# Attention's normalising factor: spread to 128 columns by GpSimd and transposed with the exponentials, instead of spread by fp32 matmuls

## The chip, the cores and the metric

The kernel runs on one core of one Trainium2 chip. Five engines work side by side: TensorE (PE; its weight loads are shown apart as PEld), VectorE (DVE), ScalarE (ACT), GpSimd (POOL) and SyncE (SP), which issues most transfers. TensorE writes only to PSUM, which has eight banks of 128 partitions x 512 fp32 columns; GpSimd cannot read PSUM. The metric is the device time of one execution in microseconds, from the first to the last instruction; shown are three executions and one more that was profiled.

## What is computed

A chain of three blocks on a batch of 4 sequences of 768 rows: a gated linear recurrence (8 heads of 48), a causal attention with 4 experts of 64 columns, of which each row takes the best two, and a layer-normed MLP of width 1536 with a residual.

```python
for t in range(S):                                   # 1: recurrence
    state = alpha[:, :, t, :, None] * state + np.einsum('bhd,bhe->bhde', k[:, :, t], v[:, :, t])
    y[:, :, t] = np.einsum('bhd,bhde->bhe', q[:, :, t], state)
...
    scores = np.where(causal, -1000000000.0, scale * (q @ k.transpose(0, 2, 1)))   # 2: for each expert e
    scores = scores - scores.max(-1, keepdims=True)
    a = np.exp(scores)
    a /= a.sum(-1, keepdims=True) + 1e-09
    ye = a @ v @ wo[e]
    out += mask[..., None] * w[:, :, kk:kk + 1] * ye
...
ch = np.maximum(xn @ w_ch1, 0.0) @ w_ch2             # 3: MLP, xn is the layer norm of x
return x + ch
```

## The kernel before

The program is written as one list of Python calls; a scheduler inside the framework then sets the order of the instructions on each engine, by its own estimate of when each can run, and sets the waits. A change in one function therefore moves instructions of others.

The main loop (line 714) runs over 48 *units* `(b, i, p)`: batch b, query chunk i of 128 rows (0 to 5; in the last batch from 5 down to 0), pair p of two experts. Around each unit `fill` (line 703) pulls in other work: in the first three batches the recurrence and the q, k, v projections of later rows (`front`), in the last batch the MLP of rows that are done (`back`). After the last unit only the MLP remains.

A unit has three parts. `scores(u)` (line 412) is called two units ahead (`LA = 2`). It multiplies q and k (three products of split operands, line 432), takes row maxima on VectorE (lines 438, 440) and exponentials on ScalarE (line 442), which also sums each row into `den`. VectorE inverts `den` (lines 446 to 449), and GpSimd multiplies it with the expert's weight from `W`: `rr`, one number for each row and expert, 128x2 (line 451).

`transp(u)` (line 454) transposes the 2(i+1) blocks of exponentials `A` with TensorE, four to a PSUM bank (line 464), and copies each bank into the buffer `at`; ScalarE does the copy, or VectorE for every fourth (lines 467, 469). `at` has two buffers (`NAT = 2`). The first group is issued ahead of the next `scores`, the rest behind it.

`av(u)` (line 472) multiplies the values `V` with the transposed blocks, so that the result has 64 rows for each expert and a column for each query row (line 487). The factor of a query row must then multiply a column. For that, two more fp32 matmuls (line 490) take `rr` with its one column repeated 64 times as weights and the identity as the moving operand, and so write the factor, spread over 64 partitions, beside the result in the same bank. ScalarE copies it out of PSUM to `rb` (line 493), VectorE multiplies the result with it (line 494), and ScalarE and GpSimd split the product into the parts `oh` and `ol` (lines 495, 496), which `wout` (line 498) multiplies with the output weights one pair of units later.

All PSUM banks come from one pool of eight, `psF`, taken in turn: a bank goes to its next user when the last reader of its contents is done.

When the third batch ends (line 716) the first rows for the MLP and its weights are loaded, and `mlp_ln` (line 581) queues the layer-norm statistics (line 590, BN_STATS of the tile `xt`) on VectorE, where they stand among the attention's instructions.

Of the kernel before, what the change touches and what calls it, by code (L numbers as in the profile page):

```python
# [10 lines left out]
F32 = mybir.dt.float32  # L11
# [4 lines left out]
AF = mybir.ActivationFunctionType  # L16
OP = mybir.AluOpType
# [7 lines left out]
NAT = 2  # L25
MB = 1.0
MB0 = -10000
TM = 4
# [27 lines left out]
B, H, S, D = 4, 8, 768, 48  # L56
DM = H * D
# [14 lines left out]
def kernel(ctx: ExitStack, tc: tile.TileContext, akq, vd, wqkv, wo, g_ln, w1, w2, out):  # L72
    nc = tc.nc
    pe, dve, act, pool, sp = nc.tensor, nc.vector, nc.scalar, nc.gpsimd, nc.sync
# [3 lines left out]
    aw = ctx.enter_context(tc.tile_pool(name="aw", bufs=3))  # L78
    sm = ctx.enter_context(tc.tile_pool(name="sm", bufs=6))
# [58 lines left out]
    ident = const.tile([128, 128], F32, name="ident")  # L138
    make_identity(nc, ident)
    for _ in range(NWU // 4):  # L140
        P = psf()
# [33 lines left out]
            load_wo()  # L175

    def load_wo():
        oraw = aw.tile([128, 2 * S], F32, name="at", bufs=NAT)[:, :2 * DM].rearrange("p (k c) -> p k c", k=2)
        sp.dma_start(oraw, wo)
        act.activation(OWH, oraw, AF.Copy)  # L180
        pool.tensor_tensor(OWL, oraw, f(OWH), op=OP.subtract)
# [230 lines left out]
    def scores(u):  # L412
        b, i, p = UN[u]
# [33 lines left out]
        else:  # L447
            dve.tensor_scalar(den, den, 1e-9, None, op0=OP.add)
        dve.reciprocal(den, den)
        rr = sm.tile([128, 2], F32, name="rr")  # L450
        pool.tensor_tensor(rr, den, W[:, i, 2 * p:2 * p + 2], op=OP.mult)
        RR[u] = rr

    def transp(u):
        b, i, p = UN[u]
        A = AA.pop(u)
        at = aw.tile([128, 2 * S], F32, name="at", bufs=NAT)
        ATT[u] = at
        blk = [(h, x) for h in range(2) for x in range(i + 1)]
        for x0 in range(0, len(blk), 4):  # L460
            g = blk[x0:x0 + 4]
            P = psf()
            for n, (h, x) in enumerate(g):
                pe.transpose(P[:, 128 * n:128 * n + 128], A[h][:, 128 * x:128 * x + 128], ident)  # L464
            cs = slice(128 * x0, 128 * (x0 + len(g)))
            if (u + x0 // 4) % TM:
                act.activation(at[:, cs], P[:, :128 * len(g)], AF.Copy)  # L467
            else:
                dve.tensor_copy(at[:, cs], P[:, :128 * len(g)])
            yield  # L470

    def av(u):
        b, i, p = UN[u]
        V = GEN[b][4]
        if p == 0:
            OT[u // 2] = (aw.tile([128, 2, 128], FR, name="oh", bufs=2), aw.tile([128, 2, 128], FR, name="ol", bufs=2))
        oh, ol = OT[u // 2]
        P = psf()
        rr = RR.pop(u)
        at = ATT.pop(u)  # L480
        O = P[:, 128:256]
        with tc.manual_schedule(engines={mybir.EngineType.PE}):
            for x in range(i + 1):
                for h in range(2):
                    e = 2 * p + h
                    c = 128 * (h * (i + 1) + x)
                    pe.matmul(O[64 * h:64 * h + 64, :], V[:, x, HD * e:HD * e + HD], at[:, c:c + 128],  # L487
                              start=(x == 0), stop=(x == i), skip_group_check=True)
            for h in range(2):
                pe.matmul(P[64 * h:64 * h + 64, :128], rr[:, h:h + 1].to_broadcast([128, 64]), ident, start=True, stop=True,  # L490
                          skip_group_check=True)
        rb = aw.tile([128, 128], F32, name="rb", bufs=2)
        act.activation(rb, P[:, :128], AF.Copy)
        dve.tensor_tensor(rb, O, rb, op=OP.mult)  # L494
        act.activation(oh[:, p], rb, AF.Copy)
        (dve if OLE else pool).tensor_tensor(ol[:, p], rb, f(oh[:, p]), op=OP.subtract)

# [324 lines left out]
```

## Time and profile before

| | us |
|---|---|
| three executions | 744.76, 748.21, 753.51 |
| median | 748.21 |
| the profiled execution, span | 749.8 |
| TensorE busy in it | 713.5 |
| VectorE, ScalarE, GpSimd busy | 447.5, 308.5, 174.5 |

In the rows further down, "busy" of TensorE counts the union of its records; a record's length includes its way through the array, so records overlap, and the start of the next one tells what one costs. fp32 matmuls appear as two records each, transposes as one. A wait is idle time of an engine, put down to what ended it. Line numbers are those of the kernel before; in the changed kernel, lines from 461 to 491 shift by up to 4, and those behind `av` by one.

### The profile page before, as it was taken

The numbers are of one execution on the slowest core, as the hardware profiler recorded it, in microseconds if no ns is written. First come the engines' busy times: TensorE is split into PE (matmuls) and PEld (weight loads), VectorE is DVE, ScalarE is ACT, GpSimd is POOL, SyncE is SP. The second block draws the span as 40 slices with busy tenths as digits, with TensorE's granted clock in tenths as the row PEclk, the third lists the DMA queues.
The fourth block names the chain that finished last, engine by engine and source line by source line (L and its number), as shares of the span: only waits on it lengthen the run. The fifth ranks groups of instructions, "written<-read, shape, count | busy, mean of one in ns | idle before, by whom it ended". The sixth has DMA issues, their size and how long they took to land.

```text
span 749.8 us, 16242 instructions
## 1 busy us (share of the span) xinstructions
PE 713.5 (95%) x6520; PEld 643.2 (86%) x6520; DVE 447.5 (60%) x1241; ACT 308.5 (41%) x879; POOL 174.5 (23%) x284
## 2 busy tenths in 40 slices
PE   7599799989989999999899999999999999999998
PEld 6488678868868788779678888999999999999997
DVE  6757787767897787766678954254245335433521
ACT  3324455545555555555567545232223123212310
POOL 4624345243464334321223221000000000000000
PEclk8688999999999999999999999999999999999999
DMA  8113424233322622211932311001100100110100
GB/s 338 71 57 115 151 68 138 98 117 121 121 97 96 208 61 83 77 41 54 323 99 79 96 43 55 22 32 43 43 11 33 43 22 22 43 43 12 32 22 22
DMA packets 30427, 60.87 MB, mean 81 GB/s; under 512 B 2960, under 2 KB 19856, under 8 KB 30352
## 3 DMA queue, kind: packets, MB, share of 16 engines
q1 hardware_dynamic: 18864, 45.68, 18.3%
q10 hardware_dynamic: 8352, 9.44, 3.6%
q0 software_dynamic: 3136, 4.72, 2.3%
q8 instruction: 51, 0.84, 0.5%
q14 instruction: 24, 0.20, 0.1%
HBM read 45.67 MB, written 14.16 MB: 80 GB/s over the span
## 4 chain that ended last, share of the span: by engine, by line
PE 69%; DVE 9%; DMA 7%; ACT 4%; POOL 3%; issue 3%; SPq 0%; ACTq 0%; POOLq 0%; DVEq 0%
PE F L631 21%; PE F L648 20%; PE F L304 5%; PE F L487 5%; PE F L432 4%; PE F L464 3%; DMA ld<-in_akq_dram 3%; PE F L505 2%; DMA raw<-in_w_dram 2%; DVE gt L199 2%; PE F L263 2%; PE F L318 2%; PE F L221 1%; ACT A L442 1%; PE F L244 1%
## 5 line engine op out<-in xcount | busy, mean ns | idle before, releaser
L635 ACT ACTIVATE hh<-F 128x256 fp32r<-128x256 f32 x144 | 55.0, 384 | 196.6 <-PE F L631 196.0
L631 PE MATMUL F<-nh,w1hl 128*128 128x256 f32 x864 | 129.0, 284 | 0.0
L631 PEld LDWEIGHTS F<-nh,w1hl 128*128 128x128 f32 x864 | 114.4, 191 | 1.7 <-issue 0.7
L648 PE MATMUL F<-w2h,hh 128*128 128x384 f32 x288 | 98.8, 343 | 0.0
L648 PE MATMUL F<-w2l,hh 128*128 128x384 f32 x288 | 97.0, 337 | 0.0
L648 PE MATMUL F<-w2h,hl 128*128 128x384 f32 x288 | 96.9, 336 | 0.0
L636 DVE SCALAR_TENSOR_TENSOR hl<-F,hh 128x256 fp32r<-128x256 f32 x144 | 60.1, 419 | 56.8 <-ACT hh L635 56.3
L442 ACT ACTIVATE A<-F,nm 128x384 f32<-128x384 f32 (+4 forms) x128 | 68.4, 541 | 52.7 <-DVE nm L440 44.4
L652 DVE TENSOR_TENSOR xt<-F,xt 128x384 f32<-128x384 f32 x24 | 13.4, 558 | 110.5 <-PE F L648 110.5
L631 PE MATMUL F<-nl,w1hl 128*128 128x256 f32 x432 | 75.5, 283 | 0.0
L487 PE MATMUL F<-at,V 128*64 128x128 f32 x672 | 62.1, 286 | 2.3 <-ACT at L467 1.6
L631 PEld LDWEIGHTS F<-nl,w1hl 128*128 128x128 f32 x432 | 62.2, 192 | 0.2 <-issue 0.2
L487 PEld LDWEIGHTS F<-at,V 128*64 128x64 f32 x672 | 41.5, 137 | 19.1 <-issue 7.5
L464 PE MATMUL F<-ident,A 128*128 128x128 f32 x336 | 54.5, 284 | 3.3 <-DVE rb L494 2.6
L648 PEld LDWEIGHTS F<-w2h,hh 128*128 128x128 f32 x288 | 54.2, 188 | 1.1 <-issue 0.8
L648 PEld LDWEIGHTS F<-w2l,hh 128*128 128x128 f32 x288 | 54.2, 188 | 0.2
L648 PEld LDWEIGHTS F<-w2h,hl 128*128 128x128 f32 x288 | 54.1, 188 | 0.2 <-issue 0.2
L464 PEld LDWEIGHTS F<-ident,A 128*128 128x128 f32 x336 | 37.9, 142 | 12.6 <-issue 5.0
L221 PE MATMUL F<-ld 48*128 48x128 f32 x384 | 37.8, 309 | 9.1 <-issue 5.1
L221 PEld LDWEIGHTS F<-ld 48*128 48x128 f32 x384 | 30.2, 203 | 15.4 <-issue 9.8
L206 POOL TENSOR_TENSOR ld<-ld,gt 128x512 f32<-128x512 f32 (+1 forms) x26 | 30.2, 1166 | 56.4 <-DVE gt L199 29.1
L467 ACT ACTIVATE at<-F 128x512 f32<-128x512 f32 (+1 forms) x72 | 38.7, 542 | 6.6 <-PE F L464 4.8
(185 smaller groups left out, 1420.9 us busy)
## 6 DMA issues: line engine op xcount, KB each, us to landing
ld<-in_akq_dram SPq DMA_DIRECT2D x24, 770.0 KB, 4.8
vb<-in_vd_dram SPq DMA_DIRECT2D x24, 256.0 KB, 2.8
raw<-in_w_dram SPq DMA_DIRECT2D x18, 256.0 KB, 2.7
wsc<-whl ACTq DMA_DIRECT2D x18, 256.0 KB, 2.4
xs<-xo ACTq DMA_DIRECT2D x24, 192.0 KB, 1.9
w1hl<-wsc POOLq DMA_DIRECT2D x4, 1152.0 KB, 14.9
xt<-xs SPq DMA_DIRECT2D x24, 192.0 KB, 2.5
raw<-in_w_dram SPq DMA_DIRECT2D x12, 384.0 KB, 3.2
```

Source lines behind the costliest of these rows:

```text
L206: (dve if GQ else pool).tensor_tensor(q[:, js], q[:, js], gt[:, js, 1:], op=OP.mult)
L221: pe.matmul(P[h][:, j], k[r, j], q[r, j], start=True, stop=True)
L304: pe.matmul(P[:, mt % 2], wt[:, k, cs], x[:, k], start=(n == 0), stop=(n == 8))
L432: pe.matmul(P[h][x], qt[rs[h], p, qs], kt[rs[h], p, pw * x:pw * x + pw], start=(n == 0), stop=(n == 2), skip_group_check=True)
L442: act.activation(A[h][:, pw * x:pw * x + pw], t, AF.Exp, bias=nm[:, h:h + 1], scale=1.0 if x < npc - 1 else -1.0, accum_out=dn2[:, h, x:x ...
L464: pe.transpose(P[:, 128 * n:128 * n + 128], A[h][:, 128 * x:128 * x + 128], ident)
L467: act.activation(at[:, cs], P[:, :128 * len(g)], AF.Copy)
L487: pe.matmul(O[64 * h:64 * h + 64, :], V[:, x, HD * e:HD * e + HD], at[:, c:c + 128], start=(x == 0), stop=(x == i), skip_group_check=True)
L631: pe.matmul(P, w[:, k, c], x[:, k], start=(n == 0), stop=(n == 8))
L635: act.activation(hh, P, AF.Relu)
L636: dve.scalar_tensor_tensor(hl, P, 0.0, f(hh), op0=OP.max, op1=OP.subtract)
L648: pe.matmul(P, x[:, o], w[:, ff], start=(ff == 0 and n == 0), stop=(ff == KF - 1 and n == 2))
```

## The change

`rr` becomes 128 x 2 x 64: GpSimd writes the product of `den` and the weight 64 times for each expert (line 451 in both kernels), into four buffers of its own. `transp` adds this tile as one more 128x128 block behind the exponentials' blocks, so that its transpose lands in 128 further columns of `at`; and the blocks are now cut into groups of nearly equal size instead of fours and a rest. The number of groups is 1, 2, 2, 3, 3, 4 for i = 0 to 5, against 1, 1, 2, 2, 3, 3. `av` loses the two spreading matmuls and the copy to `rb`; VectorE multiplies the result with the columns of `at`.

```diff
@@ -175,7 +175,7 @@
             load_wo()
 
     def load_wo():
-        oraw = aw.tile([128, 2 * S], F32, name="at", bufs=NAT)[:, :2 * DM].rearrange("p (k c) -> p k c", k=2)
+        oraw = aw.tile([128, 2 * S + 128], F32, name="at", bufs=NAT)[:, :2 * DM].rearrange("p (k c) -> p k c", k=2)
         sp.dma_start(oraw, wo)
         act.activation(OWH, oraw, AF.Copy)
         pool.tensor_tensor(OWL, oraw, f(OWH), op=OP.subtract)
@@ -447,23 +447,27 @@
         else:
             dve.tensor_scalar(den, den, 1e-9, None, op0=OP.add)
         dve.reciprocal(den, den)
-        rr = sm.tile([128, 2], F32, name="rr")
-        pool.tensor_tensor(rr, den, W[:, i, 2 * p:2 * p + 2], op=OP.mult)
+        rr = sm.tile([128, 2, 64], F32, name="rr", bufs=4)
+        pool.tensor_tensor(rr, den[:, :, None].to_broadcast([128, 2, 64]),
+                           W[:, i, 2 * p:2 * p + 2, None].to_broadcast([128, 2, 64]), op=OP.mult)
         RR[u] = rr
 
     def transp(u):
         b, i, p = UN[u]
         A = AA.pop(u)
-        at = aw.tile([128, 2 * S], F32, name="at", bufs=NAT)
+        at = aw.tile([128, 2 * S + 128], F32, name="at", bufs=NAT)
         ATT[u] = at
-        blk = [(h, x) for h in range(2) for x in range(i + 1)]
-        for x0 in range(0, len(blk), 4):
-            g = blk[x0:x0 + 4]
+        blk = [A[h][:, 128 * x:128 * x + 128] for h in range(2) for x in range(i + 1)]
+        blk.append(RR.pop(u).rearrange("p h e -> p (h e)"))
+        ng = (len(blk) + 3) // 4
+        cut = [len(blk) * n // ng for n in range(ng + 1)]
+        for y, (x0, x1) in enumerate(zip(cut, cut[1:])):
+            g = blk[x0:x1]
             P = psf()
-            for n, (h, x) in enumerate(g):
-                pe.transpose(P[:, 128 * n:128 * n + 128], A[h][:, 128 * x:128 * x + 128], ident)
-            cs = slice(128 * x0, 128 * (x0 + len(g)))
-            if (u + x0 // 4) % TM:
+            for n, a in enumerate(g):
+                pe.transpose(P[:, 128 * n:128 * n + 128], a, ident)
+            cs = slice(128 * x0, 128 * x1)
+            if (u + y) % TM:
                 act.activation(at[:, cs], P[:, :128 * len(g)], AF.Copy)
             else:
                 dve.tensor_copy(at[:, cs], P[:, :128 * len(g)])
@@ -476,9 +480,8 @@
             OT[u // 2] = (aw.tile([128, 2, 128], FR, name="oh", bufs=2), aw.tile([128, 2, 128], FR, name="ol", bufs=2))
         oh, ol = OT[u // 2]
         P = psf()
-        rr = RR.pop(u)
         at = ATT.pop(u)
-        O = P[:, 128:256]
+        O = P[:, :128]
         with tc.manual_schedule(engines={mybir.EngineType.PE}):
             for x in range(i + 1):
                 for h in range(2):
@@ -486,12 +489,8 @@
                     c = 128 * (h * (i + 1) + x)
                     pe.matmul(O[64 * h:64 * h + 64, :], V[:, x, HD * e:HD * e + HD], at[:, c:c + 128],
                               start=(x == 0), stop=(x == i), skip_group_check=True)
-            for h in range(2):
-                pe.matmul(P[64 * h:64 * h + 64, :128], rr[:, h:h + 1].to_broadcast([128, 64]), ident, start=True, stop=True,
-                          skip_group_check=True)
         rb = aw.tile([128, 128], F32, name="rb", bufs=2)
-        act.activation(rb, P[:, :128], AF.Copy)
-        dve.tensor_tensor(rb, O, rb, op=OP.mult)
+        dve.tensor_tensor(rb, O, at[:, 256 * (i + 1):256 * (i + 1) + 128], op=OP.mult)
         act.activation(oh[:, p], rb, AF.Copy)
         (dve if OLE else pool).tensor_tensor(ol[:, p], rb, f(oh[:, p]), op=OP.subtract)
```

The scheduler has set the order anew. Two places at the end of the third batch show it. First TensorE, where the kernel before has the last transposes of unit 33 (tiles `A_4858`, `A_4859`) and the first ones of unit 34 (`A_5012`), which go into the bank `F_5160`; `F_5138` is the result of unit 33, `F_5170` to `F_5172` are scores of unit 36. Before:

```order
L464 MATMUL F_5128<-ident_107,A_4858 128x128
L464 MATMUL F_5128<-ident_107,A_4859 128x128 x3
L464 MATMUL F_5134<-ident_107,A_4859 128x128 x2
L487 MATMUL F_5138<-at_5087,V0_377 64x128
L464 MATMUL F_5160<-ident_107,A_5012 128x128 x4
L487 MATMUL F_5138<-at_5087,V0_377 64x128 x6
L432 MATMUL F_5170<-KH1_1409,QH1_1407 128x384
L432 MATMUL F_5170<-KH1_1409,QL1_1408 128x384
L432 MATMUL F_5170<-KL1_1410,QH1_1407 128x384
L487 MATMUL F_5138<-at_5087,V0_377 64x128 x3
L490 MATMUL F_5138<-ident_107,rr_4888 64x128 x2
```

and after the change, where the same units have the tiles `A_4825`, `A_4826` and `A_4979`, the result `F_5105` and the bank `F_5124`:

```order
L468 MATMUL F_5093<-ident_107,A_4825 128x128 x2
L468 MATMUL F_5093<-ident_107,A_4826 128x128 x2
L468 MATMUL F_5099<-ident_107,A_4826 128x128 x3
L468 MATMUL F_5099<-ident_107,rr_4855 128x128
L490 MATMUL F_5105<-at_5053,V0_377 64x128
L468 MATMUL F_5124<-ident_107,A_4979 128x128 x3
L490 MATMUL F_5105<-at_5053,V0_377 64x128 x4
L432 MATMUL F_5133<-KH1_1400,QH1_1398 128x384
L432 MATMUL F_5133<-KH1_1400,QL1_1399 128x384
L432 MATMUL F_5133<-KL1_1401,QH1_1398 128x384
L490 MATMUL F_5105<-at_5053,V0_377 64x128 x5
```

The two matmuls with `rr` and the identity behind the last AV matmuls are gone, a transpose of `rr` stands with the last blocks instead, and the first group of unit 34 has three transposes instead of four. In both kernels the bank `F_5160` or `F_5124` held the result of unit 32 before, so these transposes wait for VectorE's multiplication of that result.

Second VectorE, at the same time, with that multiplication (`rb<-F,rb`, in the change `rb<-F,at`) and the four BN_STATS of the MLP's first rows. Before (the first BN_STATS stands three rows further up):

```order
L438 TENSOR_REDUCE mx_5102<-F 128x1
L449 RECIPROCAL den<-den 128x2
L338 TENSOR_REDUCE rank<-gt__4997 128x8
L590 BN_STATS bs<-xt 128x6
L438 TENSOR_REDUCE mx_5102<-F 128x1
L590 BN_STATS bs<-xt 128x6
L339 SCALAR_TENSOR_TENSOR ex<-rank,ex 128x8
L591 BN_AGGR mv<-bs 128x2
L494 TENSOR_TENSOR rb<-F,rb 128x128
L590 BN_STATS bs<-xt 128x6
L440 ISA F,nm<-F,cmask,mx_5102 128x384
L440 ISA nm 128x1
```

and after the change (here the first row is the first BN_STATS):

```order
L589 BN_STATS bs<-xt 128x6
L449 RECIPROCAL den<-den 128x2
L338 TENSOR_REDUCE rank<-gt__4964 128x8
L589 BN_STATS bs<-xt 128x6
L493 TENSOR_TENSOR rb<-F,at 128x128
L590 BN_AGGR mv<-bs 128x2
L589 BN_STATS bs<-xt 128x6
L440 ISA F,nm<-F,cmask,mx_5067 128x384
L440 ISA nm 128x1
L339 SCALAR_TENSOR_TENSOR ex<-rank,ex 128x8
```

Before, the multiplication stands behind the third BN_STATS, and the maxima of the next scores (`F,nm<-F,cmask`) behind the fourth. After, the multiplication stands behind the second, and the maxima behind the third.

## Rows read from the trace of the kernel before

**Rows 1.** The page: busy time with shares; TensorE in 40 slices of the span
```profile
PE 713.5 (95%) x6520; PEld 643.2 (86%) x6520; DVE 447.5 (60%) x1241; ACT 308.5 (41%) x879; POOL 174.5 (23%) x284
...
PE   7599799989989999999899999999999999999998
```

**Rows 2.** Busy us of each engine (x records) by stretch, then granted clock, DMA
```profile
75.00:470.00 395.00, 377.76 (x3982) 314.23 (x3981) 293.07 (x845) 212.03 (x622) 140.45 (x234) 0.98 0.33 105
368.00:373.00 5.00, 5.00 (x35) 3.80 (x32) 3.23 (x18) 3.37 (x14) 0.01 (x1) 0.66 1.32 389
470.00:750.00 280.00, 276.17 (x1954) 275.80 (x1952) 104.40 (x304) 70.58 (x202) 0.00 (x0) 1.00 0.09 30
```

**Rows 3.** TensorE's waits, 75 to 470 us: us in total, times, longest us
```profile
PE F L304 <- ACT xh L286: 4.2, 2, 3.5
PE F L464 <- DVE rb L494: 2.6, 2, 2.4
...
PE F L432 <- ACT at L467: 1.6, 1, 1.6
PE F L487 <- ACT at L467: 1.6, 4, 1.0
PE F L263 <- DVE rb L494: 1.1, 1, 1.1
...
PE F L244 <- ACT at L467: 0.4, 1, 0.4
PE F L487 <- DVE rb L494: 0.3, 1, 0.3
```

**Rows 4.** By line: duration ns min/median/max, first and last start us
```profile
L490 PE MATMUL F<-ident,rr x192: 272/273/421, 75.3 to 468.1; 128*64 128x128 f32 x192
L464 PE MATMUL F<-ident,A x336: 270/273/477, 63.7 to 465.4; 128*128 128x128 f32 x168
```

**Rows 5.** Timeline of TensorE, 303 to 306 us: start us, us, what xcount
```profile
303.42 0.44 PE L487 MATMUL F<-at,V 128*64 128x128 f32 x4
303.69 0.39 PE L490 MATMUL F<-ident,rr 128*64 128x128 f32 x4
304.00 1.16 PE L244 MATMUL F<-vb,kt 128*128 128x128 f32 x8
305.00 0.60 PE L464 MATMUL F<-ident,A 128*128 128x128 f32 x4
305.53 0.43 PE L263 MATMUL F<-smk,vb 128*32 128x128 f32 x8
```

**Rows 6.** Timeline of TensorE, 259 us, twelve records of AV
```profile
259.15 0.88 PE L487 MATMUL F<-at,V 128*64 128x128 f32 x12
```

**Rows 7.** Groups by line and form: xcount | busy us, mean ns | idle before
```profile
L467 ACT ACTIVATE at<-F 128x512 f32<-128x512 f32 x53 | 31.6, 598 | 6.1 <-PE F L464 4.8 <-DVE smk L225 1.1
L467 ACT ACTIVATE at<-F 128x256 f32<-128x256 f32 x19 | 7.3, 384 | 0.4 <-ACT rb L493 0.4
L508 ACT ACTIVATE xo<-F 128x384 f32<-128x384 f32 x24 | 11.9, 496 | 9.7 <-PE F L505 8.8 <-PE F L318 0.9
L493 ACT ACTIVATE rb<-F 128x128 f32<-128x128 f32 x48 | 13.2, 274 | 23.3 <-PE F L490 15.0 <-PE F L221 2.6 <-DVE whl L550 2.4
L469 DVE COPY at<-F 128x512 f32<-128x512 f32 x19 | 13.0, 685 | 1.5 <-PE F L464 1.2
L469 DVE COPY at<-F 128x256 f32<-128x256 f32 x5 | 2.1, 418 | 1.9 <-PE F L464 1.9
```

**Rows 8.** GpSimd's product and its nearest row by form; its last start
```profile
L451 POOL TENSOR_TENSOR rr<-den,W 128x2 f32<-128x2 f32 x48 | 14.6, 305 | 75.4 <-DVE den L449 59.4 <-PE F L505 4.0 <-ACT xo L508 3.6
L496 POOL TENSOR_TENSOR ol<-rb,oh 128x128 fp32r<-128x128 f32 x48 | 23.5, 489 | 60.1 <-ACT oh L495 59.9
L451 POOL TENSOR_TENSOR rr<-den,W x48: 184/197/1177, 65.1 to 461.1; 128x2 f32<-128x2 f32 x48
```

**Rows 9.** Timeline of VectorE, 359 to 368.2 us
```profile
364.34 0.56 DVE L590 BATCH_NORM_STATS2 bs<-xt 128x6 f32<-128x384 f32 x1 [1.51 <-DMA xt<-xs]
...
366.24 0.56 DVE L590 BATCH_NORM_STATS2 bs<-xt 128x6 f32<-128x384 f32 x1 [0.88 <-DMA xt<-xs]
...
366.88 0.26 DVE L494 TENSOR_TENSOR rb<-F,rb 128x128 f32<-128x128 f32 x1
367.60 0.56 DVE L590 BATCH_NORM_STATS2 bs<-xt 128x6 f32<-128x384 f32 x1 [0.47 <-DMA xt<-xs]
```

**Rows 10.** Timeline of TensorE at the same time
```profile
364.36 0.43 PE L487 MATMUL F<-at,V 128*64 128x128 f32 x2
367.19 0.65 PE L464 MATMUL F<-ident,A 128*128 128x128 f32 x4 [2.40 <-DVE rb L494]
```

## What the change will do to the time, told ahead

> **What bounds the kernel now.** I read the page first [rows 1], then the busy time by stretch [rows 2], then what TensorE waits for [rows 3], and last the timeline at the places that the change touches. TensorE is busy 95% of the span, far ahead of VectorE (60%) and ScalarE (41%); the slices show it near full from the fourth slice on. After 470 us it runs only the MLP's matmuls, 276.2 of 280.0 us busy, and no line of the change lies there: these 280 us stay. The attention units run from 75 to 470 us. In that stretch TensorE is busy 377.8 of 395.0 us, at a granted clock of 0.98, while VectorE, ScalarE and GpSimd have 293, 212 and 140 us of work [rows 2]. So in the stretch that the change touches, TensorE is the bound, and it loses 17.2 us to waits. What the change saves on another engine counts only where it shortens one of these waits; what it saves on TensorE counts nearly in full. The first 75 us (loads, the first recurrence chunks) hold at most one unit's work and stay too.
>
> **TensorE's own work.** The spreading matmuls go. They are 96 instructions and 192 records [rows 4], four records in each of 48 units. A record is listed as 273 ns long, but records overlap, so I price by starts. Twelve records of the same 64-column kind, the AV matmuls, take 0.88 us in all [rows 6]: less the last one's 0.27, that is 0.61 / 11 = 0.055 us each. 192 x 0.055 = 10.6 us go. (The four records of one unit start within 0.12 us, 0.39 - 0.27, and the next instruction follows 0.31 us after the first of them [rows 5]: four times 0.055 is 0.22, and the 0.09 left over is the change of tile shape, which the AV matmuls will have to pay when the spreading ones no longer stand behind them.)
>
> Added are 48 transposes of a 128x128 block, one record each. Four of the present ones take 0.60 us [rows 5]: (0.60 - 0.27) / 3 = 0.110 us each, so +5.3 us. Bounds: 0.110 back to back, 0.273 with no overlap at all (the listed length [rows 4]), which would make +13.1. I take 0.110, since in the built order 47 of the 48 stand right behind another transpose. The Trainium skill ("TensorE: Matmul & The Clock Gate", Part 4, PE-mode transpose) speaks against that: it gives about 275 ns for a 128x128 transpose inside a kernel. By that page the 48 would be an estimated 13.2 us and the change would lose on TensorE; the starts in [rows 5] do not agree with it as a price in a row of transposes.
>
> The order also moves. I counted over the whole built order how often TensorE goes from one tile shape to another (full 128x128; 64-column weights of AV; 32-column weights and 48 rows in the recurrence; 64 rows in the scores): 374 times before, 407 after, since the transposes now come in 120 groups instead of 96 and the scheduler puts other work between them. One change costs 0.09 us: from the spreading matmuls to the next instruction, above, and again from four transposes to the recurrence, 305.00 to 305.53 less 4 x 0.110 [rows 5]. So +33 x 0.094 = +3.1 us. Bounds: nothing, if they fall into the 17.2 us of waits, and 6.6 us, if a change costs a whole record's 0.11 us on top (33 x 0.2).
>
> Sum on TensorE: -10.6 + 5.3 + 3.1 = **-2.2 us** (between -5.3 and +9.1, the far end with transposes that do not overlap and dear changes of shape).
>
> **The chain behind AV.** ScalarE's copy of the spread factor goes: 48 x 274 ns, 13.2 us of ScalarE [rows 7]. Against it stand the wider and more numerous copies of the transposes. By the built order ScalarE has 7, 54 and 28 copies of 256, 384 and 512 columns instead of 19, 0 and 53. At 0.384, 0.496 (the 384-column copy of line 508) and 0.598 us that is 46.2 instead of 38.9 us. ScalarE gains 5.9 us net. VectorE has 1, 26 and 4 instead of 5, 0 and 19: at 0.418, 0.552 (midway between its two forms) and 0.685 us that is 17.5 instead of 15.1, +2.4 us. GpSimd's product grows from 2 to 128 columns; its nearest row is the 128-column subtraction, 489 ns against 305 [rows 8], so +8.8 us. None of the three is the bound in the stretch, and I cost them at nothing; what covers them is TensorE's 378 busy us against 293, 212 and 140. Without that cover VectorE's 2.4 us would be the price. The factor is not late either: GpSimd's last product starts at 461.1 and is 0.2 us long, the last transposes of blocks start at 465.4 [rows 4, 8]; 0.3 us more leaves about 4 us, because scores run two units ahead. Behind that product in GpSimd's queue stand the next gate products and subtractions, each 0.3 us later, on an engine with 255 idle us. The copied blocks get one more reader, VectorE's multiplication, so the buffer comes free later; its next writer is two units on, some 16 us at 395 us for 48 units. No DMA is added or moved.
>
> The last copy ahead of AV is longer in the units where a 256-column group ended the list (third and fifth query chunk, 16 units): 512 instead of 256 columns, 0.21 us, at most 3.4 us. TensorE waits only 3.6 us for these copies in all (1.6 + 1.6 + 0.4 [rows 3]), so most have other work in front; I take **+0.4 us**.
>
> **The wait that the order changes.** The longest single wait of the kernel on this chain is at 364.8 us: TensorE's next transposes need the PSUM bank of the AV result, and VectorE's multiplication that empties it is late; TensorE waits 2.40 us [rows 10]. VectorE is not slow there. Its queue holds the layer-norm statistics of the first MLP blocks, and these wait for loads [rows 9]: the third BN_STATS starts at 366.24, and only behind it comes the multiplication, at 366.88. In the changed order the multiplication stands behind the second BN_STATS, which started at 364.34 and took 0.56. Then the bank is free at about 364.90 + 0.26 = 365.2 instead of 367.19: **-2.0 us** (bounds 0 and -2.4). The third and fourth BN_STATS still wait; behind the third now stand the row maxima of the next scores, which stood behind the fourth before, so the wait does not simply reappear one instruction on. Right after this wait the granted clock over 368 to 373 us is 0.66, so part of that stretch ran at 1.2 GHz: 5 x (1 - 0.66) = 1.7 us lost [rows 2]. With a wait of 0.4 us it may stay at 2.4 GHz or drop elsewhere; I take half, **-0.9 us**. The other waits for this multiplication are 1.6 us (0.2 + 1.1 + 0.3 [rows 3]); they lose one hop of 0.27 us and ScalarE's queue: **-0.5 us**.
>
> **Sum.** -2.2 + 0.4 - 2.0 - 0.9 - 0.5 = -5.2 us. The profiled execution spans 749.8 us, 0.2% above the median of 748.2 and inside the runs (744.8 to 753.5); 749.8 - 5.2 = **744.6 us**. A measurement of this kernel tells about 1% from no change, that is, below 740.7 or above 755.7.
>
> **Rivals.** (a) *The whole gain comes*: the added changes of shape fall into waits, the clock stays up, all waits for the multiplication go: -5.3 + 0.4 - 2.4 - 1.7 - 1.6 = -10.6, 739.2 us. For it: every part has its row. Against: all must come together, and TensorE has few waits to hide 33 changes of shape in. (b) *The DMA wait only moves*: TensorE stands at the next instruction that needs VectorE behind the third BN_STATS. Then only -2.2 + 0.4 remain: 748.0 us. For it: the loads land when they land, 366.2 us and later. (c) *Transposes do not overlap*, at 0.273 us each: 7.8 us more than forecast, 752.4 us. That is the page's figure as a mechanism; the starts 0.110 us apart speak against it. (d) *Slower, by PSUM banks*: eight banks serve everything, and the transposes now take 120 instead of 96, so their takers wait more often for a reader in VectorE's queue, which is 74% busy (293 of 395). One such event is priced by the one in the trace: 2.4 us of waiting and 1.7 us of clock, 4.1 us. From the third event on (11.1 / 4.1 = 2.7) it decides: 744.6 + 12.3 = 756.9 us. Against it: all waits for a bank that hangs on the multiplication are 4.0 us today.
>
> **Chances.** Forecast 0.45, own range 741 to 749; (a) 0.27; (b) 0.11; (c) 0.05; (d) 0.12. Faster by over 1% is (a) and a tail of 0.04 of the forecast: 0.31. Slower is (d): 0.12. The rest, 0.57, is within 1%. The range of 8 in 10 reaches from 737, just under (a), to 755, above (b) and (c); it leaves out (d) and the far end of (a).
>
> **What would show it.** In the changed profile the 192 records are gone and the factor's transposes start about 0.11 us behind their neighbours (0.2 or more: (c)). TensorE's wait for the multiplication near 365 us is under 0.5 us and the clock behind it is 1.00 (else (b)). The stretch up to the last attention unit is some 5 us shorter; the MLP after it has the same length. Waits of 1 us or more for banks, on lines that had none, would mean (d). I would be wrong altogether if the moved order opens or closes waits at places where the change has nothing, above all for ScalarE's copy of the recurrence's result, 4.2 us today [rows 3]: the scheduler has reordered the whole stretch, and I have priced one place of it.

## The result, and the profile after

The changed kernel takes **752.92 us** (median of 15 runs, 749.60 to 754.53), the kernel before, run in between, 748.69 us (15 runs): a ratio of **1.0052, 95% interval 1.0031 to 1.0073**, that is 2.3 to 5.5 us slower. The forecast was 5.2 us faster: the wrong sign, though the time lies within the range of 737 to 755 and within 1% of before. Two executions of one kernel differ by more than that (744.76 to 756.0 for before), and of the two that were profiled the one of the changed kernel was the shorter: 748.8 us of span against 749.8. So what follows compares parts of the two traces, not their spans.

The page of the changed kernel, busy us with shares and records, to be held against [rows 1]:

```profile
PE 715.2 (96%) x6376; PEld 640.2 (85%) x6376; DVE 454.4 (61%) x1248; ACT 304.0 (41%) x848; POOL 184.0 (25%) x284
```

TensorE has 144 records less than before (192 gone, 48 new) and is busy 1.7 us longer. Stretches of the changed kernel, columns as in [rows 2]:

```profile
75.00:470.00 395.00, 381.16 (x3818) 313.80 (x3817) 297.16 (x847) 207.63 (x592) 146.91 (x230) 0.98 0.33 105
368.00:373.00 5.00, 5.00 (x39) 3.97 (x35) 4.85 (x21) 4.64 (x18) 0.85 (x2) 1.00 1.30 392
```

In the same 395 us TensorE now works 381.2 instead of 377.8 us, with 164 records less; the granted clock behind the stall at 365 us is 1.00 where it was 0.66. What TensorE waits for from 75 to 470 us (us in total, times, longest), to be held against [rows 3]:

```profile
PE F L304 <- ACT xh L286: 3.9, 1, 3.9
PE F L468 <- DVE smk L225: 3.7, 4, 1.6
PE F L432 <- DVE smk L225: 1.3, 1, 1.3
PE F L630 <- ACT nh L614: 1.1, 2, 0.9
...
PE F L432 <- ACT at L471: 0.6, 1, 0.6
...
PE F L468 <- DVE rb L493: 0.5, 1, 0.5
...
PE F L490 <- ACT at L471: 0.3, 1, 0.3
```

The waits for VectorE's multiplication `rb` fell from 4.0 us to 0.5 us, those for the copies `at` from 3.6 to 0.9; 3.7 + 1.3 us for `smk`, the recurrence's masked scores, came up. Neither of the two waiting lines reads `smk`: they wait for a PSUM bank that VectorE's masking (line 225) still reads. VectorE at that place, to be held against [rows 9]: the multiplication stands behind the second BN_STATS and starts at 365.13 instead of 366.88.

```profile
364.65 0.56 DVE L589 BATCH_NORM_STATS2 bs<-xt 128x6 f32<-128x384 f32 x1 [0.95 <-DMA xt<-xs]
365.13 0.27 DVE L493 TENSOR_TENSOR rb<-F,at 128x128 f32<-128x128 f32 x1
```

The AV matmuls mark the ends of the stretch that the change touches. By line (duration ns, then first and last start us), before and after:

```profile
L487 PE MATMUL F<-at,V x672: 272/273/476, 75.0 to 467.9; 128*64 128x128 f32 x168
```
```profile
L490 PE MATMUL F<-at,V x672: 272/273/421, 71.4 to 464.3; 128*64 128x128 f32 x168
```

392.9 us both times: the stretch did not become shorter, and not longer. (That it begins 3.6 us earlier in the changed kernel belongs to the first 75 us; their granted clock was 0.80 in the profiled execution before and 0.86 in the one after.) Behind it only the MLP is left. The chain that ended last, from 470 us on (start us, us, what), before and after; a row gives the time to the next row's start:

```profile
499.61 12.49 PE F L648 x72
512.10 12.94 PE F L631 x108
525.04 0.66 PE F L611 x6
525.69 12.48 PE F L648 x72
```
```profile
496.18 12.72 PE F L647 x72
508.90 12.95 PE F L630 x108
521.85 0.65 PE F L610 x6
522.51 12.72 PE F L647 x72
```

The 72 matmuls of the second MLP product, which the change does not touch, take 12.72 instead of 12.48 us a block, with the same instructions, no wait and the clock at 1.00. There are 12 blocks: 12 x 0.24 = **2.9 us**. That is inside the interval of the whole loss.

To see why the stretch stayed as long as it was, I split it by the trace. Between the first and the last AV start I add up the distances between successive starts of TensorE's records. A distance over 0.45 us counts as 0.20 us of work and the rest as a wait; of what the granted clock shows at 1.2 GHz, one half counts as work and the other as lost to the clock.

| us | stretch | work | waits | lost at 1.2 GHz |
|---|---|---|---|---|
| before | 393.0 | 368.0 | 18.1 | 6.9 |
| after | 393.1 | 372.7 | 14.6 | 5.9 |

The waits and the clock gave back 4.5 us, close to what was forecast (3.0). But TensorE's work, forecast at -2.2 us, rose by 4.7 us. So there are two questions: why a product that nobody touched became slower, and where 7 us of TensorE's work came from.

### The profile page after: what moved, and what is told of

Same layout as the page of the kernel before. It is cut to its first block, busy times and chain, and to the rows that moved or that the text cites. A ratio compares the mean times of both kernels' runs of the same rounds, so it can differ in the third digit from the quotient of the medians.

```text
span 748.8 us, 15923 instructions
## 1 busy us (share of the span) xinstructions
PE 715.2 (96%) x6376; PEld 640.2 (85%) x6376; DVE 454.4 (61%) x1248; ACT 304.0 (41%) x848; POOL 184.0 (25%) x284
## 4 chain that ended last, share of the span: by engine, by line
PE 65%; DVE 3%; DMA 2%; ACT 1%; issue 1%; POOL 0%; SPq 0%; DVEq 0%
PE F L630 21%; PE F L647 21%; PE F L490 5%; PE F L468 4%; PE F L304 3%; PE F L432 3%; PE F L504 2%; PE F L263 2%; PE F L318 2%; PE F L221 1%; PE F L610 1%; DMA ld<-in_akq_dram 1%; DMA xt<-xs 1%; PE F L244 1%; DVE gt L199 1%
## 5 line engine op out<-in xcount | busy, mean ns | idle before, releaser
L490 PE MATMUL F<-at,V 128*64 128x128 f32 x672 | 65.5, 286 | 0.6 <-ACT at L471 0.3
L468 PE MATMUL F<-ident,A 128*128 128x128 f32 x336 | 57.4, 286 | 4.9 <-DVE smk L225 3.7
L468 PEld LDWEIGHTS F<-ident,A 128*128 128x128 f32 x336 | 37.6, 142 | 15.9 <-issue 6.0
L471 ACT ACTIVATE at<-F 128x384 f32<-128x384 f32 (+1 forms) x89 | 45.4, 516 | 11.8 <-PE F L468 10.7
```

The source lines that it names most:

```text
L468: pe.transpose(P[:, 128 * n:128 * n + 128], a, ident)
```

## The experiments

"Shape changes" and "steps" below are counted in the built order. A shape change is a neighbour with another tile size of the array: 358 before, 393 after. (The prediction's 374 and 407 count a change between 48 and 64 rows as well, which use the same tile size.) A step is one use of the array by matmuls on half of it (AV and spreading with 64 columns; the scores of attention and recurrence with 64 or 48 rows): two neighbours on different halves share one (in the AV rows their records start 0.01 us apart, and the pair's four records take 4 x 0.055 = 0.22 us [rows 6]), a lone one takes one for itself.

### Addresses: e1, e2, e5, e15, e16

The change widens `at` and `rr`, so the tiles allocated behind them, the first MLP weights and the MLP's activations `nh` and `hh` among them, lie 2,880 bytes further on in SBUF; the second weights `w2h` stay where they were. e1 is the kernel before with tiles widened like that, and its own order:

```diff
-        oraw = aw.tile([128, 2 * S], F32, name="at", bufs=NAT)[:, :2 * DM]...
+        oraw = aw.tile([128, 2 * S + 128], F32, name="at", bufs=NAT)[:, :2 * DM]...
-        rr = sm.tile([128, 2], F32, name="rr")
+        rr = sm.tile([128, 2, 64], F32, name="rr", bufs=4)[:, :, 0]
-        at = aw.tile([128, 2 * S], F32, name="at", bufs=NAT)
+        at = aw.tile([128, 2 * S + 128], F32, name="at", bufs=NAT)
```

> The kernel before, instruction for instruction in the same order, with the two tiles allocated as wide as in the change, so that every tile behind them, the MLP's hidden activations among them, lies 2880 bytes further on, as in the change. Theory A (addresses): part of the change's loss has nothing to do with the factor; the second MLP product (72 matmuls of line 648), 12.48 us per half block before and 12.72 after, takes 12.72 here too, and the whole is 2.5 to 3.5 us slower than before (ratio about 1.004). Theory B (order): the loss comes from the order and the groups, the 12.72 was that one execution's; then 12.48 and a ratio of 1.000.

Measured: 750.13 us, ratio 1.0025 (0.9991 to 1.0058). The time does not tell the theories apart, since 1.000 lies inside; its chain behind the stretch does:

```profile
493.11 12.72 PE F L648 x72
505.83 12.95 PE F L631 x108
```

e2 is the change with 1,216 bytes more in front of the activations, which puts them 4,096 bytes behind their place in before; e5 is the kernel before with e1's tiles and the same 1,216 bytes, so that every tile lies as in e2 and only the order differs:

```diff
-        xt = M["x"].tile([128, 2, DM], F32, name="xt", bufs=2)
+        xt = M["x"].tile([128, 2 * DM + 152], F32, name="xt", bufs=2)[:, :2 * DM]...
```

> The changed kernel in its own order, with 1216 bytes more in front of the MLP's activations, which then lie 4096 bytes behind their place in the kernel before. Theory A: the 72 matmuls are back at 12.48 us and the kernel is 2.5 to 3.5 us faster than the changed one, about 750 us or a ratio of 1.001 to before. Theory B: as the changed kernel, ratio 1.005.

> The kernel before in its own order, with every tile at the address that it has in e2 (the wider tiles of the change, and the 1216 bytes in front of the MLP's activations). In the trace of e2 the 108 matmuls of the first MLP product took 12.60 us a block where the kernels before and after took 12.82, and the 72 of the second 12.40 as before. Theory A (addresses): 12.60 and 12.40 here too, so 12 x 0.22 = 2.6 us off, ratio 0.9965; then the change itself, e2 against this kernel, is worth nothing or costs up to 1 us. Theory C (the gain of e2 is the change's): ratio 1.000 here and e2 is 2 us better.

Measured: e2 746.39 us, 0.9966 (0.9942 to 0.9990); e5 746.05 us, 0.9966 (0.9936 to 0.9996). The chain behind the stretch, of e2 and of e5 (a row goes to the start of the next one; the 12.60 and 12.40 of the expectations go to a block's own last start, about 0.1 us less):

```profile
498.12 12.50 PE F L647 x72
510.62 12.72 PE F L630 x108
```
```profile
496.92 12.49 PE F L648 x72
509.41 12.72 PE F L631 x108
```

The order has no part in these rates: before's order shows 12.48 or 12.72 for the second product as its tiles lie, and so does the change's. At e5's addresses the first product (108 matmuls) is faster too, 12.72 instead of 12.94, which is why both kernels beat the one before. (e2's expectation of 1.001 had left that out.) **And at equal addresses the change is worth nothing that these runs can tell**, 746.39 against 746.05, each known to about 0.3%. Split as above, TensorE's work in e2 is 4.8 us more than in e5, as it is after against before.

What in the address matters? e15 and e16 are e5 with the activations another 64 and 128 bytes on (`2 * DM + 160` and `+ 168`).

> e5 with the activations of the MLP another 64 bytes further (the pad in the tile xt 160 instead of 152 numbers). If the rate of these matmuls hangs on the distance of their two operands' addresses modulo 128 bytes, both blocks are at their slower rate here: the 108 matmuls of the first product 12.8 us where e5 had 12.60, the 72 of the second 12.6 us where e5 had 12.40. If the distance modulo 128 has nothing to do with it, at least one of the two stays as in e5.

> e5 with the activations of the MLP another 128 bytes further (168 instead of 152 numbers). If the distance modulo 128 bytes decides, both blocks are as in e5: 12.60 and 12.40 us. If a longer period decides (256, 512 or 1024 bytes), at least one of them may differ.

Measured, one execution each, the chain of e15 and of e16:

```profile
493.72 12.72 PE F L648 x72
506.44 12.95 PE F L631 x108
```
```profile
497.45 12.48 PE F L648 x72
509.94 12.73 PE F L631 x108
...
523.32 12.72 PE F L648 x72
```

64 bytes made both products slow, as expected; 128 bytes brought the first back for all blocks, the second for every other block only. For the first product the place of `nh` alone does not decide: `nh` lies at 148,032 in before and at 152,128 in e5, both 64 modulo 128, and only the weights' place differs (92,736, which is 64, and 95,616, which is 0). With both operands at 64 or both at 0 modulo 128 bytes the product is slow (before, after, e1, e15), with `nh` at 64 and the weights at 0 it is fast (e2, e5, e16). Their distance, 0 or 64, fits all seven kernels; the fourth combination was not run. For the second product, where only `hh` moved, a distance of 32 is slow and 96 fast, except for every other block of e16, which this rule leaves unexplained.

### More groups, and the transpose in AV's bank: e4, e8, e3, e6, e7

e4 is the kernel before, at its own addresses, with its blocks cut into as many groups as in the change (120 instead of 96) and nothing else:

```diff
-        for x0 in range(0, len(blk), 4):
-            g = blk[x0:x0 + 4]
+        ng = (len(blk) + 4) // 4
+        cut = [len(blk) * n // ng for n in range(ng + 1)]
+        for y, (x0, x1) in enumerate(zip(cut, cut[1:])):
+            g = blk[x0:x1]
-            if (u + x0 // 4) % TM:
+            if (u + y) % TM:
```

> The kernel before with spreading matmuls and its own addresses, but the exponentials' blocks cut into as many groups as in the change (120 instead of 96) and of nearly equal size. By the prediction's sum the added changes of tile shape cost about 3 us: ratio 1.004. By the theory that more PSUM banks taken make TensorE wait: 1.005 to 1.010, with new waits of 1 us or more for banks. By theory A (addresses alone) 1.000.

Measured: 761.14 us, 1.0157 (1.0121 to 1.0194), above all three expectations. Its AV row, and its longest waits:

```profile
L489 PE MATMUL F<-at,V x672: 272/273/477, 72.2 to 475.0; 128*64 128x128 f32 x168
```
```profile
PE F L304 <- ACT xh L286: 3.4, 2, 3.1
PE F L507 <- ACT A L442: 3.0, 2, 1.6
```

The stretch is 402.8 us instead of 392.9. It isn't waits (17.5 us in all, 18.1 before): TensorE's work is 377.3 us, **9.3 more with not one matmul or transpose more**. It has 395 shape changes instead of 358 and 589 steps instead of 576.

The order of the whole list changes with every edit, so the same was done with another order: `PF1`, which paces the filling work (line 23), at 0.97 instead of 0.98, in before (e6), in e2 (e7) and in e4 (e8).

> The kernel before, same instructions and addresses, with one constant of the filling changed (PF1 0.98 to 0.97), which moves other work by a little between the units and lets the scheduler set a somewhat different order (671 of some 4300 rows on TensorE). It measures what an order alone is worth. Theory D (order): 2 to 6 us away from before, most likely slower, since the constants were chosen for the order before. Otherwise within 1.5 us, ratio 0.998 to 1.002.

> The changed kernel at the addresses of e2 with the same constant changed (0.98 to 0.97). Theory D (order): away from e2 (0.9966) by 2 to 6 us in either direction; 0.990 would show that the change is worth some 5 us in an order that suits it. Otherwise 0.995 to 0.998.

> The kernel of e4 (before, with 120 groups of transposes instead of 96; 1.0157) in another order by the same constant. If the 24 added groups cost some 12 us by themselves, by changes of tile shape, copies and banks, the ratio stays at 1.013 to 1.018. If e4 has drawn a bad order (theory D), it falls to 1.004 or less.

Measured: e6 0.9968 (0.9940 to 0.9996); e7 1.0031 (0.9992 to 1.0069); e8 1.0200 (1.0153 to 1.0246). Another order alone is worth -2 us in before, where it was expected to cost, and +5 us in e2 (0.0065 of 748 us): a forecast for this kernel can't be sharper than that. The price of the groups is no accident of one order.

e3 leaves before's groups and its copy by ScalarE as they are, and lets one transpose of the wide `rr` take the place of the two spreading matmuls in AV's bank (the MLP products run at e5's rates):

```diff
-            for h in range(2):
-                pe.matmul(P[64 * h:64 * h + 64, :128], rr[:, h:h + 1].to_broadcast([128, 64]), ident, ...)
+            pe.transpose(P[:, :128], rr.rearrange("p h e -> p (h e)"), ident)
```

> From the kernel before, one part of the change alone: GpSimd writes the factor as 128 columns and one transpose takes the place of the two spreading matmuls, but into the bank of the AV result, from which ScalarE copies it as before; groups and copies of the exponentials as before; the MLP's activations 4096 bytes further on. By the prediction's sum TensorE loses 192 records and gains 48: -10.6 + 5.3 us, and one change of tile shape per unit more (AV to the transpose), which stood between AV and the next work before; so about -5 us, ratio 0.993. If the stretch is not bound by TensorE's work: 1.000. If a reordering alone costs: up to 1.005.

Measured: 746.50 us, 0.9969 (0.9939 to 0.9999), as e5. The 48 steps of the spreading are gone, but the lone transposes raise the shape changes to 382, and TensorE's work is 366.8 us, only 0.6 less than in e5. So the extra groups are avoided and the gain is still not there.

### Halves of the array that run alone: e9, e10, e11

AV's two experts use two halves of the array, side by side if they stand side by side. The groups cut the list of blocks in places where one expert's matmul is released without the other. e9 (of e2), e10 (of e5) and e11 (of e3) list the blocks by `x` first, so that both experts of a step become ready together; e9 also cuts only between such pairs, `cut = [*range(0, 2 * i, 4), 2 * i, len(blk)]`, in as many groups as e2. The lines of e10 and e11:

```diff
-        blk = [(h, x) for h in range(2) for x in range(i + 1)]
+        blk = [(h, x) for x in range(i + 1) for h in range(2)]
-                    c = 128 * (h * (i + 1) + x)
+                    c = 128 * (2 * x + h)
```

> The changed kernel at the addresses of e2, with the blocks of exponentials in another order: the two experts' blocks of one key chunk side by side, and the groups cut between such pairs, so that both AV matmuls of a pair find their operands in the same copy. The count of groups, copies and all instructions stays. Theory E (broken pairs): in the changed order 72 of the 336 AV matmuls run without their partner on the other half of the array, and each such step costs the 0.22 us of a full pair; here 8 do, 172 steps of AV instead of 204, and TensorE changes its tile shape 379 times instead of 393. So 32 x 0.22 + 14 x 0.11 = 8.6 us less than e2, ratio 0.985 to before. If the groups cost by copies, banks or waits: as e2, 0.997.

> The kernel of e5 (before at the addresses of e2) with the same order of blocks and groups of four: AV steps, the spreading matmuls among them, 221 instead of 246, 355 changes of shape instead of 358. Theory E: 25 x 0.22 + 0.3 = 5.8 us less than e5, ratio 0.989; then e9 is 2 to 4 us faster than this kernel, as the prediction's sum says of the change once pairs stay whole. Otherwise 0.997.

> The kernel of e3 (the factor's transpose into the AV bank, 96 groups) with the same order of blocks: AV steps 173 instead of 198, 371 changes of shape instead of 382. Theory E: 25 x 0.22 + 11 x 0.11 = 6.7 us less than e3, ratio 0.988, within 2 us of e9: what e9 saves by ScalarE's copy and the shorter chain it pays back in groups. If the groups cost apart from pairs and shapes, this kernel is the fastest of the three by 5 us or more.

Measured: e9 748.90 us, 1.0013 (0.9989 to 1.0036); e10 748.90, 0.9997 (0.9973 to 1.0022); e11 **743.79, 0.9940 (0.9915 to 0.9965)**, the lowest of the versions that compute everything, though its interval overlaps that of e5. TensorE's work fell as expected, by 9.8, 6.1 and 8.5 us. But in e9 and e10 none of it became time. AV's row in e10, and its stretch:

```profile
L487 PE MATMUL F<-at,V x672: 272/273/476, 72.4 to 467.9; 128*64 128x128 f32 x168
```
```profile
75.00:470.00 395.00, 377.18 (x3953) 313.65 (x3954) 291.42 (x839) 211.33 (x619) 138.69 (x232) 0.96 0.33 105
```

395.5 us from first to last, 2.6 more than in e5, at a granted clock of 0.96 instead of 0.98: the loss at 1.2 GHz went from 8.3 to 15.9 us. In e9 the waits rose by 6.9 us and that loss by 4.7. None of the three came down to its expected ratio. e11, with 96 groups, is 5 us faster than e9, with 120, which e11's expectation names as the sign that groups cost something apart from pairs and shapes; in the split e9 has 4 us more work and 4 us more waits than e11, and what makes them was not taken apart.

### TensorE's work alone, less and more: e12, e13, e14

Is the stretch bound by TensorE at all? e12 is e5 without the spreading matmuls. ScalarE copies AV's result where it copied the factor, and the factor is left out of the output:

```diff
-            for h in range(2):
-                pe.matmul(P[64 * h:64 * h + 64, :128], rr[:, h:h + 1].to_broadcast([128, 64]), ident, ...)
-        act.activation(rb, P[:, :128], AF.Copy)
+        act.activation(rb, O, AF.Copy)
```

e13 (of e5) and e14 (of e10) have two transposes more in each unit, whose result nobody reads:

```diff
+            for n in range(2):
+                pe.transpose(P[:, 256:384], ident, ident)
```

> The order of before at e5's addresses, without the 96 spreading matmuls; nothing takes their place: ScalarE copies the head outputs themselves where it copied the spread factor, VectorE multiplies them with that, and so the factor is left out of the result. Groups, buffers and transposes stay as they are. Theory A (TensorE is the bound of the stretch from the first to the last AV matmul, so that work saved there comes off the time): 96 x 110 ns = 10.6 us less work at most (7.6 us by what the AV class lost between before and the change), so about 8 to 10 us below e5, a ratio to before near 0.985. Theory B (work saved on TensorE comes back as waits and time at the lower clock, as e9 and e10 hint): the time stays within 3 us of e5, a ratio of 0.993 to 1.000, with more waits or more time at 1.2 GHz in the stretch.

> e5 with 96 more transposes of the identity, two for each unit, into unused columns of the bank of AV's outputs, right ahead of what the spreading matmuls write: some 96 x 110 ns = 10.6 us more TensorE work in the stretch, no group and no copy more. Theory A: 10 to 12 us above e5, a ratio to before near 1.011. Theory B: the work goes into waits that are there anyway, and raises the clock's mean; at most 4 us above e5, a ratio up to 1.002.

> e10 (blocks in pairs, TensorE work 361 us of the stretch but 15.9 us lost at 1.2 GHz) with the same 96 transposes more as e13. Theory A: about 10 us above e10, a ratio to before near 1.013. Theory B: the clock stays up where it fell in e10, and the time is that of e10 within 3 us, a ratio between 0.995 and 1.004.

Measured: e12 740.29 us, 0.9896 (0.9855 to 0.9938); e13 762.91, 1.0201 (1.0171 to 1.0231); e14 758.10, 1.0139 (1.0107 to 1.0172). The rows of AV in e12, e13 and e14:

```profile
L487 PE MATMUL F<-at,V x672: 272/273/476, 73.8 to 461.7; 128*64 128x128 f32 x168
```
```profile
L489 PE MATMUL F<-at,V x672: 272/273/476, 72.8 to 480.9; 128*64 128x128 f32 x168
```
```profile
L489 PE MATMUL F<-at,V x672: 272/273/447, 73.0 to 475.6; 128*64 128x128 f32 x168
```

387.9, 408.1 and 402.6 us. Neither theory holds in both directions:

| us | against | work | waits | lost at 1.2 GHz | stretch | by the ratios | lost, all executions |
|---|---|---|---|---|---|---|---|
| e12, spreading gone | e5 | -9.3 | 0.0 | +4.3 | -5.0 | -5.2 | +2.8 |
| e9, pairs | e2 | -9.8 | +6.9 | +4.7 | +1.7 | +3.5 | +7.6 |
| e10, pairs | e5 | -6.1 | +1.0 | +7.6 | +2.6 | +2.3 | +6.4 |
| e11, pairs | e3 | -8.5 | -0.3 | +7.1 | -1.8 | -2.2 | +5.4 |
| e4, groups | before | +9.3 | -0.6 | +1.2 | +9.9 | +11.7 | +2.4 |
| e13, transposes | e5 | +13.1 | +2.1 | 0.0 | +15.2 | +17.6 | +1.7 |
| e14, transposes | e10 | +11.2 | +1.9 | -5.8 | +7.1 | +10.6 | -1.1 |

(Rounded sums.) The columns up to "stretch" come from one profiled execution of each kernel. The last two take all of them: the difference of the ratios, of 748.4 us, and (1 - granted clock) x span, averaged over a kernel's executions. That the loss rises in e9, e10 and e11 holds over all executions. In e12 it is not clear (22.5 us, with a standard deviation of 5.0 among its six, against 19.7 in e5). And the loss that e14's profile wins back is not seen over all: 25.0 us against 26.1 in e10.

Work that is added becomes time, in e14 (10.6 us for 11.2) as in e4, and in e13 even more than that (17.6 us for 13.1). Of the work that is taken away, about half becomes time in e12 (5.2 us, known to about 4, of 9.3), a quarter in e11 and nothing in e9 and e10; there the rest appears as time at 1.2 GHz, in e9 also as waits. In e12 it hangs on the clock of the single execution: two at a granted clock of 0.979 and 0.978 took 735.9 and 738.1 us, one of e5 at 0.979 took 743.1. On additions theory A was right (e14 as expected, e13 above it). On savings e12 lies between the two theories.

## Why the prediction was wrong

**TensorE's work, the step that failed.** Three terms were on record: -10.6 for the spreading matmuls, +5.3 for the transposes, +3.1 for 33 changes of shape. The first two hold. In e12 AV and spreading together fall from 66.1 to 55.1 us, -11.0; in the changed kernel the 47 transposes of `rr` in the stretch take 5.3 us, 0.11 each, and those of `A`, in more groups, 0.8 us more than before. The third was mis-sized, and a fourth was missing. Both show in the matmuls that the change leaves as they are: in the changed kernel AV and spreading together fall by 7.8 us, not by 11.0 as in e12, and the other matmuls (of the recurrence, the scores and the projections) take some 6 us more.

Ten kernels (before, after, e2 to e5, e9 to e12; eight different orders) fit one sum within 1.5 us:

work = 367.5 + 0.21 x (shape changes - 358) + 0.22 x (steps - 576) + 0.10 x (added transposes)

Four that did not go into it (e6, e8, e13, e14) come out within 2.0 us; e13, say, at 379.6 against 380.5. So by the fit a change of shape costs 0.21 us (standard error 0.03), not 0.094, and every half of the array that runs alone costs a whole step of 0.22 us. The built order has 393 shape changes instead of 358, and apart from the 48 steps of the spreading 14 steps more. By these prices the change is 48 x -0.22 + 48 x 0.10 + 35 x 0.21 + 14 x 0.22 = -10.6 + 4.8 + 7.4 + 3.1 = +4.7 us, which is what the trace shows (372.7 less 368.0; both kernels are among the ten). I had counted the shape changes (33) and priced them from two places by the extra distance to the next start only; I had not counted broken pairs at all.

That distance is only the way out of a shape: 0.20 us to the next start instead of 0.11. The first distance behind a change is longer too. In the trace of before, four transposes take 0.66 us right behind the spreading matmuls and 0.60 behind others of the full size:

```profile
202.21 0.66 PE L464 MATMUL F<-ident,A 128*128 128x128 f32 x4
...
207.97 0.60 PE L464 MATMUL F<-ident,A 128*128 128x128 f32 x4
```

So some 0.15 us of a change (0.09 + 0.06) can be read directly; what the rest of the fitted 0.21 stands for is not shown. The timeline of TensorE in the changed kernel shows the way out and a broken pair:

```profile
361.99 0.87 PE L490 MATMUL F<-at,V 128*64 128x128 f32 x10
362.79 0.45 PE L432 MATMUL F<-KH,QH 64*128 64x384 f32 x2
...
364.34 0.27 PE L468 MATMUL F<-ident,rr 128*128 128x128 f32 x1
364.54 0.43 PE L490 MATMUL F<-at,V 128*64 128x128 f32 x2
365.46 0.55 PE L468 MATMUL F<-ident,A 128*128 128x128 f32 x3 [0.48 <-DVE rb L493]
```

Ten AV records start within 0.60 us (0.87 - 0.27); the scores follow 0.20 us behind the last one. At 364.54 two records, that is one matmul, stand alone between two shapes, with the other half of the array empty; side by side with its neighbour it would share that step.

**The waits and the clock.** The place that I priced was right, the sum in part by luck. The wait for the multiplication at 365 us fell from 2.40 to 0.5 us (forecast -2.0), the clock behind it is 1.00, and no other wait for `rb` is listed (forecast -0.5). The +0.4 for longer copies was not seen: the waits for `at` fell by 2.7 us. What I had not looked at nearly cancels: 5.0 us of waits for `smk` are new, and those for the exponentials `A` fell from 5.0 to 1.1 us. In all -3.5 us of waits and -1.0 us of clock, against -2.1 and -0.9 forecast.

**"The MLP after it has the same length."** Wrong by 2.9 us, for a reason that no view of the trace before could have priced, though it could have been asked: the wider tiles move every address behind them.

**"What it saves on TensorE counts nearly in full."** Wrong for savings: nothing in e9 and e10, a quarter in e11, about half in e12. Had the work fallen by 2.2 us, e12's rate (5.0 of 9.3) would have made 1.2 us of it.

**Sum.** +4.7 - 3.5 - 1.0 = +0.2 in the stretch and +2.9 behind it, 3.1 us; measured 2.3 to 5.5. That the time lies in the range of 737 to 755 is owed to the width of the range, not to the sum.

**The rivals.** (a) fell with the shape changes. (b) fell: the DMA wait did go. (c) fell: the transpose of `rr` at 364.34 is followed after 0.20 us by another shape, and 0.11 us is the mean of its distances; the 275 ns that the Trainium skill gives ("TensorE: Matmul & The Clock Gate", Part 4, PE-mode transpose) is what the records list as a duration here, and not what one costs in a row. (d) named the right place, the 24 extra groups. Its sign was seen, waits of up to 1.6 us for banks that VectorE reads (5.0 us for `smk`), but the waits as a whole fell in the changed kernel and did not grow in e4. What cost is that the groups break up TensorE's order; that its size (12.3 us) is near the 11.7 us of e4 is chance.

The Trainium skill has a rule that I passed over ("TensorEngine Tiling (Array Packing)", Tiling Modes, Key Properties): changing the tiling mode drains TensorE. It gives no price; here one costs 0.21 us by the fit, of which 0.15 show in the starts.

**Open.** Why the clock falls when TensorE has less to do in e9 to e11 was not isolated; the granted clock of all their executions shows that it does. Why the scheduler breaks more pairs with more groups was not taken apart either.

## What to carry to other kernels

Where matmuls of several tile shapes are interleaved, count two things in the new order before summing durations: the changes of shape and the half-array matmuls without a partner; both cost about 0.2 us here, as much as one pair of the fp32 matmuls that this edit saves. Ask of every tile that changes its size what lies behind it in SBUF, and compare kernels at equal addresses before the difference is put down to the edit. In a kernel like this one, count TensorE work that is added as time, and of work that is saved not more than half, unless a run shows that the clock stays up. Read the clock from all executions: one profile of each kernel shows a clock regained in e14 that its six executions do not.

## What the runs showed of the hardware

- The rate of a run of plain matmuls hangs on SBUF addresses: 12.48 or 12.72 us for 72 matmuls with 384 columns, 12.72 or 12.95 us for 108 with 256 columns, without a wait and at a granted clock of 1.00. 64 bytes switch it. The Trainium skill ("TensorE: Matmul & The Clock Gate", Part 2, Step-by-step) says that loading the next weights takes no SBUF bandwidth from the running matmul; 2% of the rate here hang on where the two operands lie. The runs show the rate and not its reason, so they don't decide whether that sentence holds here.
- A change of tile shape on TensorE delays on both sides: the next start comes after 0.20 us instead of 0.11, and four transposes behind it take 0.66 us instead of 0.60.
- The same 96 transposes cost 2.35% (1.0201 less 0.9966, e13 on e5) in one order and 1.42% (1.0139 less 0.9997, e14 on e10) in another: a price measured in one kernel does not carry over as it is. Of the 7 us between them 2 are TensorE's work and 3 the loss at 1.2 GHz over all executions; the rest is within the noise.
